# A second pair of token tiles by seven products, five tiles beside the attention, and PSUM dealt out anew

## The chip, the cores and the metric

One Trainium2 chip, one of its cores. The time is device microseconds of that core for one execution; lower is better. In this text and in the profile, PE is TensorE (PEld its weight loads), DVE is VectorE, ACT is ScalarE, POOL is GpSimd and SP is SyncE, which issues the DMAs.

## What is computed

A random-feature attention over 8 batches of 8 heads, 576 positions of 64, and then a gated MLP on its output, 4608 tokens of 512 with a hidden width of 1536. Cut to what matters:

```python
def phi(x):
    proj = einsum('bhsd,md->bhsm', x, omega)       # 128 features
    h = proj - sum(x * x, -1, keepdims=True) / 2
    h = h - max(h, -1, keepdims=True)
    return exp(h) / sqrt(m)
q_p, k_p = phi(q * scale), phi(k * scale)
kv = einsum('bhsm,bhsd->bhmd', k_p, v); z = sum(k_p, axis=2)
x = einsum('bhsm,bhmd->bhsd', q_p, kv) / (einsum('bhsm,bhm->bhs', q_p, z)[..., None] + 1e-6)
x = x.transpose(0, 2, 1, 3).reshape(4608, 512)
g = x @ w_gate
out = (g * sigmoid(g) * (x @ w_val)) @ w_out       # the weights come as float64
```

## The kernel before

**Precision.** Each MLP operand is split into a high half (a cast, on ACT) and a low half (a subtraction, on POOL or DVE), and each product is three matmuls: high by high, high by low, low by high. The weights arrive as float64 words; `convert_all` turns 36 pieces into float32 with one ACT, five DVE and one POOL operation each and keeps them in DRAM (`wscr`).

**The attention** runs in 72 steps of two groups of 256 rows: six steps of two k groups, sixty of one q and one k group, six of two q groups. A step projects its rows with omega (`st_project`, tile `pp`, L399), takes maxima on DVE (`st_max`), exponentials on ACT (`st_exp`, L431), and adds k's features to `kvacc` (`k_accumulate`, L534). Features of q are transposed (`q_transpose`, tile `ptq`, L558) and multiplied with kv (`q_out`, tile `xt`, L600 to L635; for the first four batches by way of `q_mult`, L575). Rows for the next step are transposed in `st_transpose` (tile `pt`, L376). `q_out` writes x, column by column, as high and low halves straight into the MLP's tiles (L632, L633).

**The MLP** takes tokens in nine tiles of 512 and the hidden width in four sets of three pieces. A visit is one tile by one set (`stream`, L689): three gate products (`g`, 12 matmuls each, 512 wide), Silu of the three on ACT (L714), the four down products of the visit before (`o`, 9 matmuls each, added up in SBUF by DVE, L680), three value products (`v`, 12 each, L647). That makes 108 wide matmuls. Three rounds of tiles, 0 to 2, 3 and 4, 5 and 6, are visited this way, 28 visits, beside the attention. Tiles 7 and 8 come after it as a pair (`last_round`): for each two pieces, a 2x2 block scheme with seven products in place of eight, whose weight factors come from `load_seven` and whose x factors `t1` to `t4` from `make_t`. A pair costs six times 14 products of 6 matmuls (`a`, `c`, `d`, L832) and 8 down products of 6.

**Order.** The program is emitted in a hand-made order. In each step the list `GROUPED` (L957) runs the attention's functions, with places named SHARE at which `give` lets the MLP's generator run on; how far is set by `course`, a curve of MLP microseconds over the steps, between an upper bound (what x is whole) and a lower one (what buffers of x must be free). `MARGIN` is what is left of the MLP's visits when the attention ends. `want` sets the conversions in the same way; `need` forces them where they are late. The engines' queues are in order, so a PE instruction that waits holds up all behind it.

**PSUM** has eight banks: four for the MLP (`ps_m`), two for `pp` and, from step 26 on, `pt` and `xt` (`ps_p`), one for `ptq`, `po` and `zp` (`ps_a`), one for `kvacc`. After the attention its four go to the pair's accumulators (`ps_w`). x has four buffers for each half (`NXB`).

Of the kernel before, what the change touches and what calls it, by code (L numbers as in the profile page):

```python
# [23 lines left out]
def kernel(  # L24
# [11 lines left out]
    nc = tc.nc  # L36
# [49 lines left out]
    ps_m = ctx.enter_context(tc.tile_pool(name="ps_m", bufs=4, space=PSUM))  # L86
# [3 lines left out]
    ps_a = late.enter_context(tc.tile_pool(name="ps_a", bufs=1, space=PSUM))  # L90
    ps_k = late.enter_context(tc.tile_pool(name="ps_k", bufs=1, space=PSUM))
# [4 lines left out]
    def ps_att(name, shape):  # L96
        return ps_a.tile(shape, F32, name=name, tag="b")

# [96 lines left out]
    lower = np.minimum(lower, upper)  # L195
# [44 lines left out]
    def new_weights(f, i, pool=None):  # L240
        hi, lo = (
            (pool or wpool).tile([P, DM], F32R, name=f"w{e}{f}_{i}", tag=f"w{e}{i}") for e in ("hi", "lo")
        )
        weights[f, i] = hi, lo
# [51 lines left out]
    def load_weights(f, i, pool=None):  # L296
        need(f, i)
        new_weights(f, i, pool)
        raw = moe.tile([P, DM], F32, name=f"wraw{f}_{i}", tag="wraw", bufs=3)
        nc.sync.dma_start(raw, wscr[f, i])  # L300
        split_piece(f, i, raw)
# [67 lines left out]
    def st_transpose(n):  # L369
# [3 lines left out]
        pt = (ps_moe if n <= EARLY else ps_proj)(f"pt_{n}", [P, 2, G])  # L373
# [89 lines left out]
    def load_z(n):  # L463

        for _, b, g, gr in slots(n, "q"):
            if g == 0 and b >= BPOOL:
                assert len(converted) == 3 * NF, "the raw weights' buffers are still needed"
                zt = att.tile([P, 2, 4, M], F32, name=f"zt{b}", tag="stw")
# [80 lines left out]
    def q_transpose(n):  # L549
# [3 lines left out]
        for b, g in todo:  # L553
            ph = box.pop(("q", b, g))
            pt = (ps_moe if m < EARLY else ps_att)(f"ptq{b}_{g}", [P, 2, G])
# [3 lines left out]
            qts[b, g] = att.tile([P, 2, G], F32, name=f"qt{b}_{g}", tag="qt")  # L559
# [34 lines left out]

    xt = {}
    cols_done = [0]

    def q_out(n):
        n -= OLAG
        for _, b, g, gr in slots(n, "q"):  # L600
            po = (ps_att if n + OLAG < EARLY else ps_proj)(f"xt{b}_{g}", [P, G])
# [56 lines left out]
    at_visit = [0]  # L658

    def finished(j):  # L660

        return at_visit[0] > last_visit[j]

# [3 lines left out]
    acc = {}  # L667

    def down(j, k_, ht, wts, next_set, tt):
# [11 lines left out]
        if k_ == (NPF if j >= LASTA else NSET) - 1:  # L681
# [7 lines left out]
    def stream():  # L689

        todo = []
        for vi, (j, s_, k_) in enumerate(visits):
# [4 lines left out]
            while not avail(j):  # L697
# [3 lines left out]
                else:  # L701
                    yield None
            xs = [t[:, :, 0:w] for t in xt[j]]
# [15 lines left out]
            if final:  # L719
                load_seven(0, 0)  # L720
            while todo:
                down(*todo.pop(0))
                yield MM2
            for f in fs:
# [13 lines left out]
            if final:  # L738
                load_seven(0, 1)
            at_visit[0] = vi + 1  # L740
            wts = {f: weights[f, 2] for f in fs} if vi else None
            then = range(nxt[1] * FA, nxt[1] * FA + FA) if new_set else (0, 1) if final else None
            todo = [(j, k_, ht, wts, then, tt) for tt in range(w // P)]
        yield from last_round(todo)
# [10 lines left out]

    late_pools = {}
    sevens = {}
    ts = {}

    def load_seven(pf, i):  # L760

        win = late_pools["win"]
        raws_ = []
        for f in (2 * pf, 2 * pf + 1):
            raw = moe.tile([P, DM], F32, name=f"wraw{f}_{i}s", tag="wraw", bufs=3)
            nc.sync.dma_start(raw, wscr[f, i])
            raws_.append(raw)
# [275 lines left out]
```

## Time and profile before

| | us |
|---|---|
| median of three runs (1230.67 to 1234.53) | 1233.17 |
| the profiled execution | 1232.11 |
| its span, first to last instruction | 1229.9 |
| PE busy | 1193.3 |
| ACT, DVE, POOL busy | 624.6, 607.8, 549.3 |
| mean granted clock of PE | 0.989 |

A row of a group gives line, engine, operation, the tile written, the tiles read, shape and count, then busy time, the mean of one in ns and the idle time before, with what ended it. A row of the timeline gives start and length in microseconds, and in brackets how long the engine was idle before and what released it. Matmuls overlap in the pipeline, so a PE row's length (0.39 for a wide one) is longer than the distance between two starts. A wait is put down to whatever came last.

### The profile page before, as it was taken

The page shows a single profiled execution, that of the slowest core. Times are in us where ns is not written, and L with a number is a line of the kernel's source. Part 1 is how long each engine was busy: PE and PEld are TensorE (multiplying, and loading weights), DVE is VectorE, ACT ScalarE, POOL GpSimd, SP SyncE. Part 2 cuts the span into 40 slices and gives each one's busy share as a digit, 9 for nine tenths or more (in the row PEclk, how much of TensorE's full clock was granted, in tenths as well). Part 3 has the DMA queues.
Part 4 walks back from the last instruction along what each step waited for, and adds up shares of the span by engine and source line. Part 5 has one row for each costly group of instructions (what it writes and reads, how often), then busy time and mean ns, then how long its engine had stood idle before and what let it go on. Part 6 is the DMA issues. An engine that isn't in the chain of part 4 may idle for free. (4 is left out here: it accounts for less than half of the span.)

```text
span 1229.9 us, 18546 instructions
## 1 busy us (share of the span) xinstructions
PE 1193.3 (97%) x6777; PEld 978.9 (80%) x6777; DVE 607.8 (49%) x1192; ACT 624.6 (51%) x1387; POOL 549.3 (45%) x469
## 2 busy tenths in 40 slices
PE   6999999899999999999999999989999999999998
PEld 5888788688888888878888877877777787788886
DVE  4688767436556523433344434432334276545544
ACT  3778766543544425455754556434654423654431
POOL 3424333353444521335544654335556334656541
PEclk7899999999999999999999999999999999999999
DMA  6545644424326312232222221222111113321102
GB/s 148 138 121 141 177 137 142 117 78 142 90 68 181 90 35 73 61 78 61 72 62 61 78 56 44 61 51 60 46 42 43 43 43 77 96 52 52 52 18 69
DMA packets 158986, 100.13 MB, mean 81 GB/s; under 512 B 119824, under 2 KB 132144, under 8 KB 158896
## 3 DMA queue, kind: packets, MB, share of 16 engines
q1 hardware_dynamic: 158896, 98.95, 30.1%
q8 instruction: 54, 0.88, 0.3%
q14 instruction: 36, 0.29, 0.1%
HBM read 80.02 MB, written 18.89 MB: 80 GB/s over the span
## 5 line engine op out<-in xcount | busy, mean ns | idle before, releaser
L431 ACT ACTIVATE ph<-pp,st 128x128 f32<-128x128 f32 x576 | 158.6, 382 | 31.8 <-DVE st L420 30.9
L249 POOL TENSOR_TENSOR wlo<-wraw,whi 128x512 fp32r<-128x512 f32 x93 | 121.8, 1319 | 107.5 <-ACT whi L248 107.1
L383 POOL TENSOR_TENSOR sq<-nat 128x512 f32<-128x512 f32 x72 | 76.7, 1066 | 191.9 <-DMA nat<-in_k_dram 143.2
L680 DVE TENSOR_TENSOR acc<-o,acc 128x512 f32<-128x512 f32 x124 | 84.6, 687 | 116.5 <-PE o L656 116.2
L656 PE MATMUL o<-whi,hh 128*128 128x512 f32 x336 | 135.5, 403 | 3.8 <-ACT hh L733 2.0
L647 PE MATMUL v<-xh,whi 128*128 128x512 f32 x336 | 134.5, 400 | 0.7 <-DVE acc L680 0.7
L647 PE MATMUL g<-xh,whi 128*128 128x512 f32 x336 | 134.6, 401 | 0.0
L656 PE MATMUL o<-whi,hl 128*128 128x512 f32 x336 | 132.3, 394 | 2.3 <-POOL hl L734 2.3
L647 PE MATMUL g<-xl,whi 128*128 128x512 f32 x336 | 131.7, 393 | 0.5 <-DVE xl L633 0.5
L656 PE MATMUL o<-wlo,hh 128*128 128x512 f32 x336 | 131.6, 392 | 0.0
L647 PE MATMUL v<-xh,wlo 128*128 128x512 f32 x336 | 131.4, 391 | 0.0
L647 PE MATMUL g<-xh,wlo 128*128 128x512 f32 x336 | 131.3, 392 | 0.0
L647 PE MATMUL v<-xl,whi 128*128 128x512 f32 x336 | 131.2, 391 | 0.0
L734 POOL TENSOR_TENSOR hl<-sl,hh 128x512 fp32r<-128x512 f32 x84 | 110.5, 1319 | 41.8 <-ACT hh L733 41.3
L417 DVE TENSOR_REDUCE st<-pp 128x4 f32<-128x512 f32 x144 | 93.5, 684 | 54.2 <-PE pp L399 54.2
L733 ACT CAST hh<-sl 128x512 fp32r<-128x512 f32 x84 | 52.1, 626 | 108.7 <-DVE sl L730 108.5
L248 ACT CAST whi<-wraw 128x512 fp32r<-128x512 f32 x93 | 57.4, 625 | 92.2 <-PE v L647 54.1
L410 DVE TENSOR_REDUCE st<-sq 128x8 f32<-128x512 f32 x72 | 49.1, 682 | 105.0 <-POOL sq L383 105.0
L399 PE MATMUL pp<-omT,x 64*128 64x128 f32 x1152 | 98.3, 296 | 2.4 <-ACT x L384 1.2
L399 PEld LDWEIGHTS pp<-omT,x 64*128 64x128 f32 x1152 | 81.2, 196 | 22.8 <-issue 13.9
L730 DVE TENSOR_TENSOR sl<-v,sl 128x512 f32<-128x512 f32 x84 | 57.3, 686 | 72.3 <-PE v L647 70.0
L494 POOL TENSOR_TENSOR jk<-ph,zt 128x512 f32<-128x512 f32 x32 | 41.1, 1290 | 103.6 <-ACT ph L431 86.8
(200 smaller groups left out, 2448.3 us busy)
## 6 DMA issues: line engine op xcount, KB each, us to landing
wraw<-wscr SPq DMA_DIRECT2D x93, 256.0 KB, 2.7
wscr<-wc SPq DMA_DIRECT2D x36, 256.0 KB, 2.2
out_dram<-acc SPq DMA_DIRECT2D x72, 128.0 KB, 2.4
nat<-in_k_dram SPq DMA_DIRECT2D x64, 128.0 KB, 3.3
v<-in_v_dram SPq DMA_DIRECT2D x64, 128.0 KB, 3.4
nat<-in_q_dram SPq DMA_DIRECT2D x64, 128.0 KB, 2.7
st<-in_moe_w_gate_dram SPq DMA_DIRECT2D x12, 512.0 KB, 5.1
st<-in_moe_w_val_dram SPq DMA_DIRECT2D x12, 512.0 KB, 4.4
```

The lines of the kernel that those rows point to most:

```text
L248: nc.scalar.copy(hi, raw)
L249: nc.gpsimd.tensor_tensor(lo, raw, hi.bitcast(F32), op=ALU.subtract)
L383: nc.gpsimd.tensor_tensor(sq, nat, nat, op=ALU.mult)
L399: nc.tensor.matmul(pp[hh][:, i, c, :], x[r, i, c * P : (c + 1) * P], omT[r], start=True, stop=True)
L417: nc.vector.tensor_reduce(st[:, 1, :, :, hh], pp[hh], axis=AX.X, op=ALU.max, negate=True)
L431: nc.scalar.activation(ph[:, c, hh * M : (hh + 1) * M], pp[hh][:, i, c, :], AF.Exp, bias=st[:, 3, i, c, hh : hh + 1], scale=1.0,)
L647: nc.tensor.matmul(ps, a_[:, ws], b_[:, c, :], start=n == 0, stop=n == 3 * NC - 1)
L656: nc.tensor.matmul(ps, a_[:, ts_], b_, start=first and n == 0, stop=last and n == 2)
L680: nc.vector.tensor_tensor(a_, po, a_, op=ALU.add)
L730: nc.vector.tensor_tensor(h, pv, h, op=ALU.mult)
L733: nc.scalar.copy(hh, h)
L734: nc.gpsimd.tensor_tensor(hl, h, hh.bitcast(F32), op=ALU.subtract)
```

## The change

Tiles 0 to 4 are visited beside the attention, in two rounds, 20 visits. Tiles 5 and 6 and then 7 and 8 are pairs by seven products, twelve pair visits; the second pair runs over the pieces backwards, so that the last weights serve twice. The x of tiles 3 to 8 goes to DRAM as plain float32 (`x_dram`); tiles 3 and 4 are fetched again before their round (`fetch_x`), the first pair's factors are made from DRAM as the attention ends (`first_x`), the second pair's raw factors are prepared ahead (`next_x`) and split during the last half visit of the first pair (`split_x`). With that x needs three buffers, the lower bound on the course and the forced `give` in `q_out` go, and the margin is 45.

PSUM: three banks for the MLP; one bank (`ps_b`) for `pt`, for the first `xt` of a step, and for the second `ptq` where a step has two; `pp` has its two banks to itself. Afterwards the pair has five banks and its down products three. `q_out` moves up between the halves of `k_accumulate`. Weights of the pair are fetched some products ahead (`weights_work`).

```diff
-    ROUNDS = [range(0, 3), range(3, 5), range(5, 7)]
-    LASTA, LASTB = 7, 8
-    MARGIN = 25.0
-    NXB = 4
+    ROUNDS = [range(0, 3), range(3, 5)]
+    PAIRS = [(5, 6), (7, 8)]
+    MARGIN = 45.0
+    NXB = 3
...
-    ps_m = ctx.enter_context(tc.tile_pool(name="ps_m", bufs=4, space=PSUM))
+    ps_m = ctx.enter_context(tc.tile_pool(name="ps_m", bufs=3, space=PSUM))
+    ps_b = late.enter_context(tc.tile_pool(name="ps_b", bufs=1, space=PSUM))
+    def ps_tr(name, shape):
+        return ps_b.tile(shape, F32, name=name, tag="t")
...
-        lower[n] = max([0.0] + [cum[last_visit[j - NXB] + 1] for j in begun if j >= NXB and begun[j] <= n])
...
-        pt = (ps_moe if n <= EARLY else ps_proj)(f"pt_{n}", [P, 2, G])
+        pt = ps_tr(f"pt_{n}", [P, 2, G])
...
-            pt = (ps_moe if m < EARLY else ps_att)(f"ptq{b}_{g}", [P, 2, G])
+            pt = (ps_moe if m < EARLY else ps_tr if i else ps_att)(f"ptq{b}_{g}", [P, 2, G])
...
-            po = (ps_att if n + OLAG < EARLY else ps_proj)(f"xt{b}_{g}", [P, G])
+            po = (ps_att if n + OLAG < EARLY or i else ps_tr)(f"xt{b}_{g}", [P, G])
...
+                if j in x_dram:
+                    xo = att.tile(list(src.shape), F32, name=f"xo{b}_{g}_{j}", tag="xo", bufs=3)
+                    nc.scalar.copy(xo, src)
+                    nc.sync.dma_start(x_dram[j][:, pr, o : o + w], xo)
+                    continue
                 if j not in xt:
-                    while j - NXB >= 0 and not finished(j - NXB):
-                        assert give(1), "the MLP waits for x, and x for the MLP"
...
+    def fetch_x(j):
+        xt[j] = [xres.tile([P, NPAIR, T], F32R, name=f"x{e}{j}", tag=f"x{e}") for e in "hl"]
+        for c in range(NC):
+            raw = moe.tile([P, T], F32, name=f"xraw{j}_{c}", tag="wraw", bufs=3)
+            nc.sync.dma_start(raw, x_dram[j][:, c, :])
+            hi, lo = (t[:, c] for t in xt[j])
+            nc.scalar.copy(hi, raw)
+            nc.gpsimd.tensor_tensor(lo, raw, hi.bitcast(F32), op=ALU.subtract)
...
+            if nxt and nxt[0] not in xt and avail(nxt[0]) and last_visit[nxt[0] - NXB] < vi:
+                fetch_x(nxt[0])
...
+    def split_x(name):
+        hi, lo = factors[name]
+        nc.scalar.copy(hi, ahead[name])
+        nc.vector.tensor_tensor(lo, ahead[name], hi.bitcast(F32), op=ALU.subtract)
...
+                    if new_x and i == 1:
+                        split_x(PROD[n][1])
...
         lambda n: k_accumulate(n, 0),
+        q_out,
         lambda n: k_accumulate(n, 1),
...
         lambda n: st_transpose(n + 1),
-        q_out,
         q_mult,
...
-        ("ps_w", tc.tile_pool(name="ps_w", bufs=4, space=PSUM)),
+        ("ps_w", tc.tile_pool(name="ps_w", bufs=5, space=PSUM)),
...
-    late_pools["mt"] = make_t()
-    for _ in late_pools["mt"]:
-        give(1.0)
+    new_factors()
+    for _ in first_x():
+        give(1.5)
```

What this makes of the order is shown at three places. First PE before, in step 65, at the end of the first visit of tile 5 (`v` and `o` are the value and down products of that same visit, `hh` and `hl` the split halves):

```order
L647 MATMUL v_2_8238<-xh_6028,whi_1_7332 128x512
L647 MATMUL v_2_8238<-xl_6029,whi_1_7332 128x512
L647 MATMUL v_2_8238<-xh_6028,wlo_1_7333 128x512
L656 MATMUL o_0_0_8256<-whi_2_7490,hh_0_8171 128x512
L656 MATMUL o_0_0_8256<-wlo_2_7491,hh_0_8171 128x512
L656 MATMUL o_0_0_8256<-whi_2_7490,hl_0_8172 128x512
L656 MATMUL o_0_0_8256<-whi_2_7496,hh_1_8234 128x512
```

And PE now, in step 59, where the second round begins with tile 3 (`xh_6292` and `xl_6293` are that tile's fetched halves, `ptq`, `kvacc` and `xt` the attention's):

```order
L566 MATMUL ptq_6_6384<-ident,ph_57_6131 128x128 x4
L542 MATMUL kvacc_0_6391<-v_97,ph_57_6136 128x65 x2
L623 MATMUL xt_5_6394<-qt_5_6238,kvr_0_4492 64x256 x2
L542 MATMUL kvacc_0_6391<-v_97,ph_57_6136 128x65 x2
L659 MATMUL g_9_6428<-xh_6292,whi_0_5136 128x512
L659 MATMUL g_9_6428<-xl_6293,whi_0_5136 128x512
L659 MATMUL g_9_6428<-xh_6292,wlo_0_5137 128x512
```

Before, the down products stand right behind the last value product of their own visit; now a gate product of the next tile follows, and `xt` stands between the halves of `kvacc`.

The second place is PE before where `pt` and `xt` of a step stood together between MLP units, in step 58:

```order
L647 MATMUL v_5_7298<-xh_4864,wlo_1_6705 128x512
L376 MATMUL pt_7312<-ident,nat_6932 128x128 x4
L613 MATMUL xt_4_7322<-qt_4_7080,kvr_0_5421 64x256 x2
L647 MATMUL g_0_7338<-xh_2566,whi_0_7113 128x512
L647 MATMUL g_0_7338<-xl_2567,whi_0_7113 128x512
```

The same place now, in step 59, between the second and the third gate product:

```order
L659 MATMUL g_10_6441<-xh_6292,whi_0_5142 128x512
L659 MATMUL g_10_6441<-xl_6293,whi_0_5142 128x512
L659 MATMUL g_10_6441<-xh_6292,wlo_0_5143 128x512
L385 MATMUL pt_6455<-ident,nat_6092 128x128 x4
L659 MATMUL g_11_6465<-xh_6292,whi_0_5148 128x512
```

`pt` stands there alone, in a bank of its own.

The third place is new: DVE in the last half visit of the first pair, where the second pair's factors are split (`b11lo`, `t1lo` and so on), between additions into the seven products' sums (`late_8880`), gating products (`sl1k`) and the down products' additions (`acc`):

```order
L841 TENSOR_TENSOR b11lo<-late_8876,b11hi 128x1024
L697 TENSOR_TENSOR acc_0_9285<-o_4_0_10241,acc_0_9285 128x512
L841 TENSOR_TENSOR t1lo<-late_8876,t1hi 128x1024
L971 TENSOR_TENSOR late_8880<-c_1_10221,late_8880 128x512
L841 TENSOR_TENSOR t2lo<-late_8877,t2hi 128x1024
L953 TENSOR_TENSOR sl1k<-late_8880,sl1k 128x512
L841 TENSOR_TENSOR b22lo<-late_8877,b22hi 128x1024
L697 TENSOR_TENSOR acc_1_9312<-o_4_1_10270,acc_1_9312 128x512
L971 TENSOR_TENSOR late_8880<-a_1_10220,late_8880 128x512
L841 TENSOR_TENSOR t3lo<-late_8878,t3hi 128x1024
```

The additions that empty `c` and `a` stand behind three and four of the wide subtractions.

More of the change, by code (lines that the diff above doesn't have):

```diff
@@ L294, in need, with load_weights, fetch @@
             tick()
-    def load_weights(f, i, pool=None):
+    def load_weights(f, i):
         need(f, i)
[L298 to L301, printed above, removed]
+        fetched = fetch((f,), i)
+        new_weights(f, i)
+        split_piece(f, i, fetched[0])
+    def fetch(fs, i):
+        raws_ = []
+        for f in fs:
+            raw = moe.tile([P, DM], F32, name=f"wraw{f}_{i}", tag="wraw", bufs=3)
+            nc.sync.dma_start(raw, wscr[f, i])
+            raws_.append(raw)
+        return raws_
     omT = const.tile([P, M], F32, name="omT")
@@ L466, in load_z @@
             if g == 0 and b >= BPOOL:
-                assert len(converted) == 3 * NF, "the raw weights' buffers are still needed"
-                zt = att.tile([P, 2, 4, M], F32, name=f"zt{b}", tag="stw")
+                zt = att.tile([P, 2, 4, M], F32, name=f"zt{b}", tag="zt")
                 for a2 in range(2):
@@ L595 @@
     xt = {}
+    x_dram = {j: dram.tile([P, NPAIR, T], F32, name=f"xs{j}") for j in range(NXB, len(TILES))}
     cols_done = [0]
@@ L875, in plus @@
                 def plus(n, ps, name):
[L876 removed]
+                    o = sl[n] if i == 0 else kp[:, 3]
                     nc.vector.tensor_tensor(o, ps, keep[name], op=ALU.add)
                     use(n, o)
[L880 to L883 removed]
```

272 lines of the change are left out of this document (156 added, 116 removed).

## The prediction

> **What bounds the kernel now.** I read the page's first part, then the busy time by stage, then what TensorE waits for, then the chain that ended last.
>
> ```profile
> span 1229.9 us, 18546 instructions
> PE 1193.3 (97%) x6777; PEld 978.9 (80%) x6777; DVE 607.8 (49%) x1192; ACT 624.6 (51%) x1387; POOL 549.3 (45%) x469
> ```
>
> TensorE is busy 97% of the span, no other engine, its own overlapping weight loads aside, over 51%. That is a mean over stages, so the stages follow: columns are length, then busy time of PE, weight loads, DVE, ACT and POOL, the granted clock, DMA. The cuts are the attention alone (0 to 130), its steps with little MLP (to 240), the MLP's forced stretch (to 440), attention with MLP between (to 950), the end.
>
> ```profile
> 0.00:130.00 130.00, 113.62 (x990) 102.28 (x991) 91.21 (x222) 89.96 (x271) 48.86 (x61) 0.91 0.57 141
> 130.00:240.00 110.00, 102.95 (x685) 85.19 (x684) 77.78 (x176) 68.97 (x167) 39.70 (x32) 1.00 0.51 145
> 240.00:440.00 200.00, 199.56 (x996) 165.10 (x995) 99.28 (x167) 86.87 (x166) 87.28 (x67) 1.00 0.34 101
> 440.00:950.00 510.00, 505.71 (x2898) 405.72 (x2897) 200.02 (x423) 267.22 (x585) 237.13 (x207) 1.00 0.23 58
> 950.00:1230.00 280.00, 271.50 (x1216) 220.62 (x1214) 139.47 (x206) 111.58 (x201) 136.33 (x105) 1.00 0.21 57
> ```
>
> From 130 us on PE has work in every stage and the others are at 71% or less, so the time is TensorE's instruction stream plus its few waits. Those, longest first in total:
>
> ```profile
> PE pt_om L312 <- DMA om<-in_omega_dram: 4.9, 1, 4.9
> PE pt L376 <- ACT ph L431: 3.8, 4, 2.5
> ...
> PE o L656 <- POOL hl L734: 2.3, 2, 1.3
> PE o L656 <- ACT hh L733: 2.0, 1, 2.0
> PE o L656 <- ACT sl L714: 1.7, 1, 1.7
> ...
> PE o L656 <- POOL hl0s L862: 0.9, 1, 0.9
> PE v L647 <- DVE acc L680: 0.7, 1, 0.7
> PE a L832 <- DVE c L877: 0.3, 1, 0.3
> ```
>
> A matmul removed is therefore worth its pitch. Busy times are pipelined and overlap, so the pitch comes from starts, in the chain that ended last (start, length, what):
>
> ```profile
> 1068.68 1.38 PE a L832 x6
> ...
> 1140.79 1.36 PE c L832 x6
> ```
>
> Between these two lie 53 groups of six matmuls 512 wide: 72.11 us by 318 is 0.227 us each.
>
> **The change part by part.** The sum is made against the profiled execution, 1232.11 us, which is its span of 1229.9 and 2.2 around it; the median of the runs, 1233.17, is 1.1 above it.
>
> *Matmuls.* A pair of tiles costs 2 x 4 visits x 108 = 864 wide matmuls in the plain way, and 6 x (14 x 6 + 48) = 792 by seven products. A second pair saves 72, all on the bound engine: 72 x 0.227 = **-16.3**. The order counts 3816 before and 3744 now.
>
> *The MLP that caught up with the attention.* Before, tiles 5 and 6 run beside the attention, and the first visit of their round ends before x of tile 6 is whole (step 66). The loop then takes the down products straight after the value products, whose split halves are not ready:
>
> ```profile
> 825.24 0.39 PE L656 MATMUL o<-wlo,hh 128*128 128x512 f32 x1
> 827.65 0.50 PE L656 MATMUL o<-whi,hh 128*128 128x512 f32 x1 [2.02 <-ACT hh L733]
> ...
> 829.70 1.22 PE L656 MATMUL o<-whi,hl 128*128 128x512 f32 x2 [1.31 <-POOL hl L734]
> 830.72 0.63 PE L656 MATMUL o<-whi,hh 128*128 128x512 f32 x1
> 831.14 0.63 PE L656 MATMUL o<-wlo,hh 128*128 128x512 f32 x1
> ...
> 833.18 0.60 PE L376 MATMUL pt<-ident,nat 128*128 128x128 f32 x4
> ```
>
> From 825.24 to 833.18 eleven matmuls start in 7.94 us where 11 x 0.227 = 2.50 would do: 5.4 lost, part of it after the waits at a pitch of 0.42 us (830.72 to 831.14), a slowed clock. The new list of five tiles asks for tiles 3 and 4 only after twelve visits, in step 59, when they have been whole since steps 43 and 48; no down product follows a value product of its own visit there. **-5.4**, at least 0.
>
> *One bank for the transposes of q and k.* From step 26 on pt took a bank of the projections, which the exponentials must first empty:
>
> ```profile
> 219.60 0.66 PE L376 MATMUL pt<-ident,nat 128*128 128x128 f32 x4 [2.47 <-ACT ph L431]
> ```
>
> Now it has its own, shared with xt, which is read out half a step earlier. Of the 3.8 us in the list of waits I take **-3**, between 0 and -3.8: next late there is ACT itself. *In the last steps, with two q groups each*, the second ptq and the first xt share that bank, so xt waits for a copy like this one:
>
> ```profile
> 611.41 0.58 ACT L560 COPY qt<-ptq 128x512 f32<-128x512 f32 x1 [0.57 <-PE ptq L558]
> ```
>
> Six such steps, 0 to 0.6 us each with what the scheduler puts between: 0 to +4, taken **+1**.
>
> *Three banks for the MLP instead of four.* Nothing of before shows three, but it shows when each bank was emptied. I set the start of each of 325 accumulators (g, v, o) against the end of the read-out of the third one before it, instead of the fourth. In 314 the read-out had ended. In eleven it had not, by 13.2 us together; these are the two largest:
>
> ```profile
> 303.78 0.39 PE L647 MATMUL v<-xh,whi 128*128 128x512 f32 x1
> ...
> 305.87 1.28 DVE L680 TENSOR_TENSOR acc<-o,acc 128x512 f32<-128x512 f32 x2
> ```
> ```profile
> 1023.59 0.50 PE L656 MATMUL o<-whi,hh 128*128 128x512 f32 x1 [1.66 <-ACT sl L714]
> ...
> 1025.91 2.48 DVE L680 TENSOR_TENSOR acc<-o,acc 128x512 f32<-128x512 f32 x4
> ```
>
> The value product at 303.78 would need the second of two additions, ending at 306.5; the down product at 1023.59 the first of four, ending at 1026.5. Eight of the eleven lie between 291 and 412 us, where DVE converts weights in bursts and hardly any attention lies between the MLP's units, three at the entry to the pair stage, none between 440 and 950:
>
> ```profile
> 350.00:400.00 50.00, 50.00 (x246) 41.62 (x246) 32.48 (x56) 22.32 (x43) 21.40 (x17) 1.00 0.41 121
> ```
>
> The new order spreads those conversions over steps 34 to 46 with attention in every gap, which takes most of them away and adds a few. 0 to +13.2; nearer the lower half: **+5**.
>
> *Edits with one answer.* Before step 25 the projections and ptq share three banks where they and pt shared four, so the cover is the same; xt moved up between the halves of the kv products, a fourth qt buffer and zt's own buffer change no count; 0, and if the early steps lose their cover, some tenths of a us in each of 25.
>
> *x through DRAM.* For tiles 3 to 8 one ACT copy replaces cast and subtraction, and a DMA goes onto SP's queue behind it, ahead of loads issued three steps early: nothing on PE. Tiles 3 and 4 come back in four chunks each, 256 KB, one cast and one POOL subtraction a chunk:
>
> ```profile
> L249 POOL TENSOR_TENSOR wlo<-wraw,whi 128x512 fp32r<-128x512 f32 x93 | 121.8, 1319 | 107.5 <-ACT whi L248 107.1
> ...
> L248 ACT CAST whi<-wraw 128x512 fp32r<-128x512 f32 x93 | 57.4, 625 | 92.2 <-PE v L647 54.1
> ...
> wraw<-wscr SPq DMA_DIRECT2D x93, 256.0 KB, 2.7
> ```
>
> 2.7 + 0.6 + 4 x 1.3 = 8.5 us, under three value products (36 x 0.227 = 8.2) and an attention group: 0 to +3 a tile, **+1** for both.
>
> *Entering the first pair.* Before, four waits there sum to 3.6 (sl 1.7, hl0s 0.9, acc 0.7, c 0.3). DVE now does 22 operations instead of 24, beneath 45 us of MLP instead of 25: -3.6 to +3.6, **-1**.
>
> *Entering the second pair* is new: while the last half visit runs, seven factors of 128x1024 are split again, each a cast and a DVE subtraction. The nearest DVE rows are half as wide, alone and beside a POOL instruction:
>
> ```profile
> 998.41 0.69 DVE L822 TENSOR_TENSOR t0l<-t1f,t0h 128x512 fp32r<-128x512 f32 x1
> ...
> 1002.43 1.77 DVE L822 TENSOR_TENSOR t1l<-t2f,t1h 128x512 fp32r<-128x512 f32 x1
> ```
>
> So 1.4 to 2.5 each, 10 to 17 us, and eleven other operations of 0.69 make 17 to 25 in a half visit of 11 x 6 x 0.227 = 15.0. Each factor is used only a half visit later, but product 4 waits for an addition queued behind those splits: 0 to +5, **+2**. [...]
>
> Sum: -16.3 - 5.4 - 3 + 1 + 5 + 1 - 1 + 2 = -16.7. Span 1213.2, execution 1215.4, median **1216.5**.
>
> **The rivals.**
>
> *Nothing new waits.* No bank wait, all old waits gone: -16.3 - 5.4 - 3.8 - 3.6 = -29.1, **1204**. For it: DVE and ACT are half idle. Against: conversions still come in bursts of 15 operations. Chance 0.17.
>
> *The seams take it back.* Banks at their bound (+13.2), second pair +5, fetched tiles +6, two-q steps +4 against -16.3 and -5.4: +6.5; with half of the last two +1.5, so **1235**, no change that a measurement of this kernel can tell (0.3%, some 3.7 us). For it: each has its row. Against: all must come together. 0.11.
>
> *Three banks stop PE in every visit (slower).* With three gates in three banks, the first down product needs the first Silu finished, where before it had the fourth bank. ACT may have exponentials and a table load ahead:
>
> ```profile
> 600.12 0.39 PE L656 MATMUL o<-whi,hh 128*128 128x512 f32 x1
> ...
> 599.80 0.91 ACT L431 ACTIVATE ph<-pp,st 128x128 f32<-128x128 f32 x3
> 600.73 1.28 ACT L714 ACT_TABLE_LOAD   x1
> 602.02 0.60 ACT L714 ACTIVATE sl<-g 128x512 f32<-128x512 f32 x1
> ```
>
> Had that been the first Silu, the down product at 600.12 would start 2.5 us late. A bank fewer moves each need forward by one accumulator, so where four just sufficed a visit loses 9 x 0.227 = 2.04 us: 20 visits, +40.8 in place of +5, **1252**. It decides from (21.7 + 3.7)/20 = 1.3 us a visit. Against it: none of the eleven late read-outs lies in the mixed stage, which most resembles the new one. Two short waits close together also slowed the clock at 830 (a pitch of 0.42), which would raise the price. 0.10. [...]
>
> **How the numbers follow.** Forecast 0.62 (1209 to 1224), rivals 0.17, 0.11, 0.10. Range 1204 to 1231: from the first rival to within the second. Faster than 1229.5: 0.62 + 0.17 + 0.03 = 0.82; within 0.3%: 0.08; slower: 0.10.
>
> **What would show it.** Right: 3744 wide matmuls, no PE wait of 2 us and no clock dip where the second round ends, fewer than 10 us of PE waiting on acc, sl or v's read-out, a pair stage at 0.227 throughout save the second pair's entry. Wrong: o or v waiting on ACT sl or DVE acc visit after visit, or a PE share under 95% after 240 us.

## The result, and the profile after

| | before | after |
|---|---|---|
| median, us (lowest to highest) | 1231.92 (1228.93 to 1234.53), 4 runs | 1218.27 (1217.01 to 1221.51), 4 runs |
| ratio after to before | | 0.9892, 95% interval 0.9872 to 0.9912 |
| the profiled execution, us | 1232.11 | 1217.01 |
| its span, us | 1229.9 | 1214.9 |
| wide matmuls | 3816 | 3744 |

The kernel became 1.1% faster; 1216.5 had been forecast. The page after has the same shape as before: TensorE at 97%, and no other engine above 54%, its own overlapping weight loads (79%) aside:

```profile
span 1214.9 us, 18839 instructions
PE 1173.3 (97%) x6705; PEld 965.4 (79%) x6705; DVE 646.2 (53%) x1231; ACT 656.6 (54%) x1461; POOL 584.9 (48%) x500
```

The last three of the same stages in the trace of after (length, busy time of PE, weight loads, DVE, ACT and POOL, the granted clock, DMA):

```profile
...
240.00:440.00 200.00, 189.11 (x1138) 154.90 (x1137) 124.89 (x228) 107.48 (x238) 94.40 (x75) 0.98 0.44 124
440.00:950.00 510.00, 503.24 (x2717) 404.70 (x2716) 216.88 (x402) 271.75 (x575) 270.57 (x231) 1.00 0.30 79
950.00:1215.00 265.00, 260.14 (x1147) 214.75 (x1145) 136.93 (x209) 113.77 (x198) 130.14 (x102) 1.00 0.20 53
```

One row has changed its nature. Before, PE was busy for 199.56 of the 200 us from 240 to 440; now it is for 189.11, and DVE has 124.89 us to do there where it had 99.28. The list of what PE waits for, in the trace of after, says on whom:

```profile
PE pp L408 <- ACT x L393: 5.6, 7, 2.1
...
PE pt L385 <- ACT xo L638: 4.4, 3, 2.7
...
PE ptq L566 <- DVE xn L593: 3.2, 2, 1.8
PE a L874 <- DVE sl2k L971: 3.2, 1, 3.2
PE pt L385 <- DVE xl L645: 2.5, 3, 1.9
...
PE a L874 <- ACT late L967: 1.5, 2, 1.2
PE o L668 <- ACT sl L733: 1.4, 1, 1.4
PE v L659 <- DVE acc L697: 1.3, 2, 1.1
PE o L668 <- DVE acc L697: 1.2, 1, 1.2
```

`pt` no longer waits for the exponentials `ph`; it waits for `xo` and `xl`, the two read-outs of `xt`, which now shares its bank. The waits on hh and hl of the visit's own, where the second round ended, are gone. The three banks show as sl and acc: 1.4 + 1.3 + 1.2 = 3.9 us.

To compare kernels I cut their traces at the same steps of the attention, not at the same times; the start of a step is taken from its copy of x out of `pt` (L393). The idle time of PE that ends on another engine or a DMA is added up for each part:

| steps | before | after |
|---|---|---|
| 0 to 24 | 16.1 | 13.8 |
| 24 to 35 | 7.4 | 4.8 |
| 35 to 50 | 0.2 (242 to 589 us) | 11.1 (237 to 456 us) |
| 50 to 68 | 3.8 | 2.0 |
| 68 to the end | 3.6 | 4.9 |
| all | 31.1 | 36.6 |

Steps 35 to 50 are where the change gives something back. They lasted 347 us and last 219 now, because the MLP no longer has to run ahead there to free a buffer of x; the same attention and the same conversions of weights stand in a shorter stretch. A second sum, the start of the last wide matmul less 0.2268 us for each wide matmul, holds all that isn't wide matmuls on time: 359.3 us before, 360.9 after. So the 72 matmuls (16.3 us) are the whole gain, and everything else comes out at +1.6 us, of gains and losses that the experiments take apart in part.

### The profile page after: what moved, and what is told of

Same layout as the page of the kernel before. It is cut to its first block, busy times and chain, and to the rows that moved or that the text cites. A ratio compares the mean times of both kernels' runs of the same rounds, so it can differ in the third digit from the quotient of the medians.

```text
span 1214.9 us, 18839 instructions
## 1 busy us (share of the span) xinstructions
PE 1173.3 (97%) x6705; PEld 965.4 (79%) x6705; DVE 646.2 (53%) x1231; ACT 656.6 (54%) x1461; POOL 584.9 (48%) x500
## 4 chain that ended last, share of the span: by engine, by line
PE 59%; DVE 5%; DMA 3%; POOL 2%; issue 2%; ACT 1%; SPq 0%; POOLq 0%; DVEq 0%; ACTq 0%
PE o L668 19%; PE a L874 10%; PE v L659 7%; PE g L659 7%; PE c L874 5%; PE d L874 2%; PE pp L408 2%; PE kvacc L542 2%; PE xt L623 1%; PE ptq L566 1%; DMA nat<-in_k_dram 1%; PE pt L385 1%; DMA first_b<-xs 1%; POOL jk L502 0%; DVE wc L276 0%
## 5 line engine op out<-in xcount | busy, mean ns | idle before, releaser
L426 DVE TENSOR_REDUCE st<-pp 128x4 f32<-128x512 f32 x144 | 92.7, 682 | 24.2 <-PE pp L408 23.7
L668 PE MATMUL o<-whi,hh 128*128 128x512 f32 x240 | 97.1, 405 | 2.6 <-ACT sl L733 1.4
L408 PEld LDWEIGHTS pp<-omT,x 64*128 64x128 f32 x1152 | 77.8, 196 | 26.4 <-issue 13.8
L659 PE MATMUL v<-xh,whi 128*128 128x512 f32 x240 | 96.7, 403 | 1.3 <-DVE acc L697 1.3
L659 PE MATMUL g<-xh,wlo 128*128 128x512 f32 x240 | 95.1, 396 | 0.0
L668 PE MATMUL o<-wlo,hh 128*128 128x512 f32 x240 | 94.3, 393 | 0.0
L668 PE MATMUL o<-whi,hl 128*128 128x512 f32 x240 | 94.1, 392 | 0.2 <-POOL hl L756 0.2
L659 PE MATMUL v<-xh,wlo 128*128 128x512 f32 x240 | 94.0, 392 | 0.0
L659 PE MATMUL v<-xl,whi 128*128 128x512 f32 x240 | 93.7, 390 | 0.0
L280 POOL TENSOR_TENSOR wc<-st,wc 128x512 f32<-128x512 f32 x36 | 47.5, 1321 | 80.2 <-DVE wc L278 27.8
L865 POOL TENSOR_TENSOR wlo<-s,whi 128x512 fp32r<-128x512 f32 x44 | 64.8, 1489 | 34.6 <-DVE late L971 11.7
L865 POOL TENSOR_TENSOR wlo<-wraw,whi 128x256 fp32r<-128x256 f32 (+1 forms) x44 | 45.1, 1025 | 72.0 <-ACT whi L864 71.9
```

Of the source, the lines that this page charges most:

```text
L408: nc.tensor.matmul(pp[hh][:, i, c, :], x[r, i, c * P : (c + 1) * P], omT[r], start=True, stop=True)
L426: nc.vector.tensor_reduce(st[:, 1, :, :, hh], pp[hh], axis=AX.X, op=ALU.max, negate=True)
L659: nc.tensor.matmul(ps, a_[:, ws], b_[:, c, :], start=n == 0, stop=n == 3 * NC - 1)
L668: nc.tensor.matmul(ps, a_[:, ts_], b_, start=first and n == 0, stop=last and n == 2)
L865: nc.gpsimd.tensor_tensor(lo, src_, hi.bitcast(F32), op=ALU.subtract)
```

## The experiments

Each kernel is one edit away from before, from after, or from another experiment. Line numbers in their traces are shifted by a few lines. Waits are those of PE in the profiled execution, in us.

| kernel | median | ratio to before (95%) | all waits | steps 35 to 50 |
|---|---|---|---|---|
| after | 1218.27 | 0.9892 (0.9872 to 0.9912) | 36.6 | 11.1 |
| psum_only | 1229.56 | 0.9983 (0.9963 to 1.0003) | 33.2 | 8.1 |
| pair_only | 1235.02 | 1.0040 (1.0014 to 1.0066) | 44.0 | 14.0 |
| pair_three | 1238.28 | 1.0063 (1.0036 to 1.0089) | 45.2 | 13.8 |
| q_late | 1232.61 | 1.0007 (0.9986 to 1.0027) | 45.2 | 13.4 |
| pair_qup | 1243.24 | 1.0100 (1.0071 to 1.0130) | 55.2 | 19.7 |
| xt_att | 1244.60 | 1.0095 (1.0069 to 1.0121) | 47.7 | 18.3 |
| q_first | 1220.08 | 0.9915 (0.9889 to 0.9940) | 39.5 | 8.0 |
| conv_light | 1202.01 | 0.9765 (0.9733 to 0.9797) | 32.7 | 1.0 |
| no_catchup | 1226.48 | 0.9956 (0.9937 to 0.9975) | 27.2 | 0.2 |
| prep_late | 1221.79 | 0.9911 (0.9883 to 0.9938) | 38.0 | 9.1 |
| prep_pool | 1221.86 | 0.9910 (0.9877 to 0.9943) | 36.7 | 11.4 |
| combo1 | 1266.12 | 1.0267 (1.0229 to 1.0304) | 66.0 | 24.3 |

### The two halves of the change, apart

**psum_only** is before with the PSUM dealt out anew and `q_out` moved up, and with no second pair:

```diff
-    ps_m = ctx.enter_context(tc.tile_pool(name="ps_m", bufs=4, space=PSUM))
+    ps_m = ctx.enter_context(tc.tile_pool(name="ps_m", bufs=3, space=PSUM))
+    ps_b = late.enter_context(tc.tile_pool(name="ps_b", bufs=1, space=PSUM))
...
-        pt = (ps_moe if n <= EARLY else ps_proj)(f"pt_{n}", [P, 2, G])
+        pt = ps_tr(f"pt_{n}", [P, 2, G])
...
-            po = (ps_att if n + OLAG < EARLY else ps_proj)(f"xt{b}_{g}", [P, G])
+            po = (ps_att if n + OLAG < EARLY else ps_tr)(f"xt{b}_{g}", [P, G])
```

> The kernel before with PSUM dealt out as now, and nothing else but q_out moved up: three banks for the MLP, one for pt and xt, five and three banks in the pair stage. Theory A (the new deal costs: late read-outs with three banks up to 13.2 us, most in the MLP's forced stretch, and pt now waits for the read-out of xt, against 3.8 us of waits on the exponentials that go): slower than before by 3 to 10 us, 1235 to 1242, with PE waits on acc, sl and v's read-out of 4 us or more between 240 and 440 us. Rival B (the deal is the gain: with pp's banks to itself the early steps run ahead, as the changed kernel reached step 24 6 us earlier): faster by 3 to 8 us, 1224 to 1229, with step 24 reached near 124 us.

**pair_only** is the opposite: after with the three lines above, the pair's banks and the place of `q_out` as they were before.

> The changed kernel with PSUM as before (four banks for the MLP, pt and xt in the projections' banks, four banks for the pair) and q_out in its old place: the second pair alone. Theory A: 72 matmuls and the stall at the second round's end go (-21.7), the new PSUM deal isn't paid: 1208 to 1214, and the PE waits on acc and sl between 250 and 440 us (3.7 us in the changed kernel) are gone, with those on xo and xl. Rival B: without the deal's gain 1221 to 1226.

Theory A was right about the waits in both, and about the time in neither. In psum_only PE waits for the third bank where the late read-outs had been found. The longest of these waits, at 302.63 us, is this row; 1.9 and 1.3 us follow at 381.31 and 389.04, 7.8 in all:

```profile
PE v L651 <- DVE acc L684: 4.6, 1, 4.6
```

Rival B fell as well: step 24 starts at 128.5 us, where it starts at 125.5 in before and at 124.1 in after. In pair_only the waits on acc and sl are gone, with those of `pt` on xo and xl. Still the deal by itself is worth nothing that can be told (0.9983, interval up to 1.0003), and the second pair by itself is slower than before (1.0040), although it has its 72 matmuls fewer. Only together do they give 1.1%. In the list of waits of pair_only one row stands out:

```profile
PE pt L381 <- ACT ph L436: 18.5, 11, 4.8
```

Before, the same transposes in the same banks waited 3.8 us for the same exponentials. What changed is what lies over them: 13.1 of the 18.5 us fall in steps 35 to 50, where before had no such wait, and these steps are shorter by a third. Their granted clock is 0.96, where it was 1.00.

**no_catchup** prices the stall at 825 us in before: the MLP hands out no early down products while x of tile 6 is not whole.

```diff
-                if todo:
+                if todo and j != 6:
```

> The kernel before with one edit: while x of tile 6 isn't whole, the MLP hands out nothing, where it handed out the down products of the visit just done. Theory A (the stall at 825 us costs 5.4): no wait on hh and hl and no clock dip there, 4 to 6 us faster than before. Rival B (the attention step left without MLP work costs as much, since PE then waits for the step's own chain): within 2 us of before.

The stall and the dip of the clock behind it (granted 0.50 from 831 to 833 us in the trace of before) are gone; 0.9956 of 1230.83 is 5.4 us less (3.1 to 7.8).

**pair_three** takes the fourth MLP bank from pair_only and leaves it unused.

```diff
-    ps_m = ctx.enter_context(tc.tile_pool(name="ps_m", bufs=4, space=PSUM))
+    ps_m = ctx.enter_context(tc.tile_pool(name="ps_m", bufs=3, space=PSUM))
```

> The second pair with PSUM as before, but three banks for the MLP during the attention and the pair stage, one bank left unused: it prices the fourth bank alone. Theory A (three banks cost little once attention lies between the MLP's units; what made the old deal slow here are the 18.5 us for which pt waits for exponentials): within 4 us of the old deal's 1235, that is 1233 to 1240, and pt still waits 12 us or more. Rival B (the MLP's banks matter as much as my bound of 13.2): 1243 to 1250, with over 8 us of PE waits on acc, sl and v's read-out.

1238.28 against 1235.02: the fourth bank is worth some 3 us; the intervals, 1.0036 to 1.0089 and 1.0014 to 1.0066, overlap, so it may be less. No visit after visit of waiting came with it.

### Who makes PE wait in steps 35 to 50

**conv_light** is after with one DVE operation for each converted piece of weights instead of five. It leaves out the clamp and the bit operations, so that the weights are other numbers; the MLP's work is otherwise the same.

```diff
-            nc.vector.tensor_scalar(u, u, E_LO, E_HI, op0=ALU.max, op1=ALU.min)
...
-            nc.vector.tensor_scalar(ui, ui, 3, 0x3FFFFFFF, op0=ALU.logical_shift_left, op1=ALU.bitwise_and)
...
-            nc.vector.scalar_tensor_tensor(ri, ri, -0x40000000, ui, op0=ALU.bitwise_and, op1=ALU.bitwise_or)
...
-            nc.vector.tensor_single_scalar(ui, ri, -0x800000, op=ALU.bitwise_and)
```

> The changed kernel with one DVE operation in place of five for each converted weight piece (the conversion's range and bit operations are left out, so the weights are other numbers). Theory A (the 10.9 us of PE waits between 255 and 431 us come from conversions queued on DVE and ACT in steps 34 to 46): those waits fall under 4 us and the time by 7 to 12, to 1206 to 1211. Rival B (they come from three banks and the shared bank of pt and xt, whatever DVE does): the waits stay over 7 us and the time falls by under 4.

The waits of these steps go from 11.1 to 1.0 us and the time to 1202.01. So it is DVE's part of the conversions that makes PE wait there; DVE is busy for 93.36 us of these steps, in after for 133.42. The time falls by 16 us, more than these 10. The start is not where it comes from: the first wide matmul starts at 125.1 us, that of after at 130.8, but at step 35 conv_light is only 0.6 us ahead (236.2 and 236.8), since `pt` waits 6.8 us for xl before it. Steps 35 to 50 then take 204.6 us in place of 218.9. Of these 14.3 us 10.1 are waits, and the rest goes with a granted clock of 1.00 where after has 0.98.

**combo1** tries to make use of that in a kernel that still computes everything: the clamp goes to POOL (and the subtractions of prep_pool, below, too).

```diff
-            nc.vector.tensor_scalar(u, u, E_LO, E_HI, op0=ALU.max, op1=ALU.min)
+            nc.gpsimd.tensor_scalar(u, u, E_LO, E_HI, op0=ALU.max, op1=ALU.min)
```

> The changed kernel with the preparing subtractions on POOL and, of the five DVE operations of a weight's conversion, the first one (the clamp) on POOL as well. Theory A (the waits in steps 35 to 50, 11.1 us, come from DVE's queue): DVE has some 36 operations less, those waits fall to 5 to 9 and the time by 4 to 8 with the second pair's wait, to 1210 to 1214. Rival B (the conversion's chain or POOL takes its place): those waits stay at 10 or more, the time at 1214 to 1220.

It is the slowest of all, 1266.12. The groups of POOL and of DVE in its trace show why (busy time, mean ns; idle time before them and on what):

```profile
L270 POOL TENSOR_SCALAR wc<-wc 128x512 f32<-128x512 f32 x36 | 70.6, 1961 | 43.9 <-ACT wc L268 43.8
```
```profile
L272 DVE TENSOR_SCALAR wc<-wc 128x512 int32<-128x512 int32 x36 | 33.3, 924 | 75.9 <-POOL wc L270 73.4 <-DMA xs<-xo 2.5
```

On DVE, in the trace of after, the clamp is this group:

```profile
L270 DVE TENSOR_SCALAR wc<-wc 128x512 f32<-128x512 f32 x36 | 22.2, 617 | 20.9 <-ACT wc L268 20.7
```

An operation of 617 ns became one of 1961, and the next one on DVE waits 73.4 us in total for it, with the attention's maxima behind. DVE's own work fell, from 646.2 to 629.4 us; its queue got later, and not in steps 35 to 50 alone: of the 54.6 us between the two profiled executions 33.3 are lost by step 35. (The other edit in this kernel is harmless by itself, as prep_pool shows below.)

### The bank and the place of q_out

In after, `pt` waits for `xt`'s read-out, 6.9 us. **xt_att** gives `xt` another bank, that of `ptq` and `po`:

```diff
-            po = (ps_att if n + OLAG < EARLY or i else ps_tr)(f"xt{b}_{g}", [P, G])
+            po = ps_att(f"xt{b}_{g}", [P, G])
```

> The kernel after, with one edit: every xt goes to the bank of ptq, po and zp, so that pt shares its bank with nothing but the second ptq of the last steps. In the kernel after pt waits 4.4 us for the copy of xt to xo and 2.5 us for the subtraction to xl. Theory A: these 6.9 us are the price of the shared bank; they go, and PE gains 3 to 6 us with the slowed clock behind them: 1212 to 1215. Theory B: the price is the lateness of ACT and DVE among the conversions, whichever bank xt has; the waits move to ptq and po (ptq or po on xo or xl, 5 us or more together), and the time stays within 1216 to 1222. Between the two the sum of all PE waits decides: 36.6 in the kernel after, under 32 by A, over 34 by B.

**q_late** puts `q_out` back behind the next step's transposes:

```diff
         lambda n: k_accumulate(n, 0),
-        q_out,
         lambda n: k_accumulate(n, 1),
...
         lambda n: st_transpose(n + 1),
+        q_out,
         q_mult,
```

> The kernel after, with one edit undone: q_out stands behind the next step's transposes again, as before the change, instead of between the halves of the kv products. The prediction put this move at nothing. Theory A: the move is what makes one bank for pt and xt possible; with xt right behind pt in the same bank, xt must wait for the copy of pt (some 0.6 us on ACT behind what is queued there) in up to 48 steps, where MLP products in between do not hide it: xt shows waits on x of 4 us or more in total, and the time is 1222 to 1232. Theory B: the MLP's products lie between in nearly all steps, pt no longer waits for xo and xl, and the two balance: 1214 to 1221.

In xt_att both theories fell: the waits did move, but to `xt` itself, which stands right behind `ptq` in the bank and waits for the copy qt, 19.9 us in total, and the time is 1244.60. In q_late A was right: 19.3 us of waits on x, and 1232.61, just past its range. The lists of waits, first of xt_att, then of q_late:

```profile
PE xt L616 <- ACT qt L568: 12.7, 7, 3.6
PE xt L623 <- ACT qt L568: 7.2, 2, 4.1
```
```profile
PE xt L616 <- ACT x L393: 10.9, 7, 4.3
PE xt L623 <- ACT x L393: 8.4, 6, 5.3
```

One of these waits, followed back in the timeline of q_late. PE stops at 369.96 with 8 of 12 matmuls of `g` to go, because `xt` needs the bank of `pt`:

```profile
367.56 0.60 PE L385 MATMUL pt<-ident,nat 128*128 128x128 f32 x4
...
369.56 0.40 PE L659 MATMUL g<-xh,whi 128*128 128x512 f32 x1
374.28 0.44 PE L616 MATMUL xt<-ident,xn 128*128 128x128 f32 x2 [4.32 <-ACT x L393]
```

ACT empties `pt` only after the step's eight exponentials, and has itself been idle for 3.30 us, waiting for DVE:

```profile
371.58 2.17 ACT L440 ACTIVATE ph<-pp,st 128x128 f32<-128x128 f32 x8 [3.30 <-DVE st L429]
373.59 0.63 ACT L393 COPY x<-pt 128x512 f32<-128x512 f32 x1
```

And DVE comes to the maxima (L426) and to L429 among operations of the conversion (L270 to L278, two of them shown):

```profile
366.97 0.68 DVE L274 SCALAR_TENSOR_TENSOR st<-st,wc 128x512 int32<-128x512 int32 x1
...
368.02 1.28 DVE L426 TENSOR_REDUCE st<-pp 128x4 f32<-128x512 f32 x2
369.22 0.68 DVE L278 SCALAR_TENSOR_TENSOR wc<-st,wc 128x512 f32<-128x512 uint32 x1
...
370.23 1.25 DVE L429 SCALAR_TENSOR_TENSOR st<-st 128x8 f32<-128x8 f32 x1
```

So the rule of these three kernels: a bank that PE needs again, and that is given back behind the step's exponentials, is waited for by 18 to 31 us in total, 13.1 to 19.7 of it in steps 35 to 50. In pair_only it is `pp`'s bank, which the exponentials read; in q_late it is `pt`'s, whose copy stands behind them on ACT. In after neither `pt` nor `xt` stands behind them: `xt` follows a copy of x that was made half a step earlier, and the copy of x that does stand behind them is wanted only by the next step's `pp`, which waits 1.3 us for it in steps 35 to 50.

**pair_qup** closes the square: pair_only with `q_out` moved up.

```diff
         lambda n: k_accumulate(n, 0),
+        q_out,
         lambda n: k_accumulate(n, 1),
...
-        q_out,
         q_mult,
```

> pair_only (the second pair with the PSUM of before: four MLP banks, pt and xt in pp's two banks) plus the move of q_out between the halves of the kv products, as the kernel after has it. pair_only took 1235.0 and had PE waiting 18.5 us in pt for the exponentials; the kernel after with q_out in its old place took 1232.6. Theory A: the move alone is what was worth 14 us, in either deal, since it puts work between the transposes and the next step: pt's 18.5 us fall under 8 and the time comes to 1217 to 1224, so that the new deal of PSUM would be worth little. Theory B: the move pays only with the bank of pt's own; here pt still needs a bank of pp, which the exponentials empty, wherever xt stands: 14 us or more of waits for ph remain and the time is 1229 to 1238, so that deal and move are one edit worth some 14 us together and nothing apart.

B was right, and too mild: 1243.24. With a bank of `pp`, `xt` itself now waits for the exponentials, earlier in the step than `pt` did:

```profile
PE xt L619 <- ACT ph L436: 16.6, 10, 5.5
PE xt L612 <- ACT ph L436: 14.1, 8, 3.6
```

| second pair, with | q_out in its old place | q_out moved up |
|---|---|---|
| the PSUM of before | 1235.0 (pair_only) | 1243.2 (pair_qup) |
| the PSUM of after | 1232.6 (q_late) | 1218.3 (after) |

By itself the new PSUM gives 2.4 us, which can't be told from nothing (the intervals of pair_only and q_late overlap), and the move loses 8.2; together they give 16.7. **q_first** goes one place further in the same direction, ahead of `q_transpose`:

```diff
+        q_out,
         q_transpose,
         lambda n: k_accumulate(n, 0),
-        q_out,
         lambda n: k_accumulate(n, 1),
```

> The kernel after with q_out moved up once more, ahead of q_transpose instead of between the halves of the kv products, so that xt is read out earlier still before the next pt needs its bank. Theory A: pt's waits for xo and xl (4.4 and 2.5 us in the kernel after) come from the shortness of that gap; they fall under 2 us and the time is 1212 to 1217. Theory B: the gap was taken from the other side: xt now comes sooner after x is read out of the bank and after xn is made, so xt waits on x or xn by 4 us or more, as xt waited 19.3 us on x with q_out in its old place, and the time is 1218 to 1226.

The waits of `pt` on xo and xl fall from 6.9 to 0.7 + 1.2 = 1.9 us, as A had it, but the time doesn't: 1220.08, and the interval overlaps that of after. The list of its waits shows what came in their place:

```profile
PE pp L408 <- ACT x L393: 8.3, 8, 2.1
...
PE ptq L566 <- POOL hl L756: 2.8, 1, 2.8
PE o L668 <- DVE acc L697: 2.7, 1, 2.7
PE o L668 <- ACT sl L733: 2.6, 2, 2.2
```

Neither theory's row: xt on x does not appear, xt on xn is 2.5. In steps 35 to 50 all waits fall from 11.1 to 8.0 us, and elsewhere they rise from 25.5 to 31.5. It looks as if the lateness is DVE's and ACT's and shows at the next places once the shared bank is relieved; no run shows that by itself.

### The entry to the second pair

In after PE waits 3.19 us at 881.77 for an addition on DVE. This is in the first pair, 138 us before the second pair's first product (1019.28). DVE's timeline there:

```profile
873.29 1.28 DVE L850 TENSOR_TENSOR s<-wraw 128x256 f32<-128x256 f32 x1 [5.25 <-DMA wraw<-wscr]
...
875.62 1.28 DVE L829 TENSOR_TENSOR late<-late,late 128x512 f32<-128x512 f32 x2
876.83 1.28 DVE L829 TENSOR_TENSOR late<-late 128x512 f32<-128x512 f32 x2
878.03 0.68 DVE L971 TENSOR_TENSOR sl0k<-c,late 128x512 f32<-128x512 f32 x1
878.63 2.48 DVE L829 TENSOR_TENSOR late<-late,late 128x512 f32<-128x512 f32 x4
881.04 0.68 DVE L971 TENSOR_TENSOR sl2k<-a,late 128x512 f32<-128x512 f32 x1
```

These are the eight subtractions of `next_x` (L829), which prepare the second pair's raw factors. They come in one block, and the last of their loads was issued late: it stood on SP's queue behind three fetches of weights, which took 8.92 us to issue while SP waited for their buffers:

```profile
861.97 8.92 SPq L308 DMA_DIRECT2D wraw<-wscr  x3
870.94 0.43 SPq L825 DMA_DIRECT2D late<-xs  x1
```

**prep_late** lets nine more units pass before the subtractions and one between each two.

```diff
-        yield
+        for _ in range(9):
+            yield
...
                 nc.vector.tensor_tensor(ahead[o][:, c], ahead[a][:, c], ahead[b][:, c], op=ALU.subtract)
                 yield
+                yield
```

> The changed kernel with the eight DVE subtractions that prepare the second pair's factors begun a pair visit later and one to every second down product, their DMAs where they were. Theory A (the 3.2 us wait of product 4 at 881 us is due to the eight subtractions in one block ahead of its addition): that wait goes, the time falls by 2.5 to 4, to 1214 to 1216. Rival B (it is due to the weights' DMA, late behind the 2 MB for those factors, on which DVE stood for 5.25 us just before): the wait stays over 2 us, the time within 1.5 of the changed kernel's.

Inconclusive: the wait on sl2k is 3.2 us as before. The block on DVE stayed whole; the emission was spread, the instructions weren't. That fits the late load as the reason for the block; no run moves the load alone.

**prep_pool** puts the eight on POOL.

```diff
-                nc.vector.tensor_tensor(ahead[o][:, c], ahead[a][:, c], ahead[b][:, c], op=ALU.subtract)
+                nc.gpsimd.tensor_tensor(ahead[o][:, c], ahead[a][:, c], ahead[b][:, c], op=ALU.subtract)
```

> The changed kernel with the eight subtractions that prepare the second pair's factors on POOL instead of DVE. Theory A (product 4 waits 3.2 us because four of them stand ahead of its addition on DVE): the wait on sl2k goes, the time falls by 2 to 4, to 1214 to 1217. Rival B (DVE is late because it stood 5.3 us for the next weights' DMA): the wait stays over 2 us and the time with it.

The wait on sl2k is gone, although DVE stood 5.25 us for a load just before, as in after; so the block on DVE was its cause. But another wait comes half a visit later. POOL has the eight subtractions until 888.3 us and frees the weights' buffers later, DVE then stands 12.35 us for a fetch of weights, and PE waits for DVE's next addition:

```profile
892.41 0.63 DVE L850 TENSOR_TENSOR s<-wraw 128x256 f32<-128x256 f32 x1 [12.35 <-DMA wraw<-wscr]
```
```profile
897.45 0.50 PE L874 MATMUL a<-t4hi,whi 128*128 128x512 f32 x1 [1.79 <-DVE late L971]
```

From step 68 on the waits fall from 4.9 to 3.1 us, but the stretch takes 515.6 us in both kernels: seven of the matmuls behind the new wait start 0.43 us apart. The median can't tell the two apart: 1221.86, 0.9910 (0.9877 to 0.9943).

None of the kernels that compute the whole is faster than after.

## Why the prediction was right, and where its steps failed

- **Matmuls, -16.3: right.** 3744 wide ones, and in the pair stage six still take 1.36 us from start to start, 0.227 each:

```profile
911.98 1.36 PE a L874 x6
913.34 1.36 PE o L668 x6
```

- **The MLP that caught up, -5.4: right**, in cause and in size: no_catchup measured -5.4 (-3.1 to -7.8), and after has no such stall.
- **One bank for the transposes, -3: the step that failed.** Where it looked, in steps 24 to 35, the waits did fall by 2.6 us. But it priced the bank by the 3.8 us that the trace of before shows, a wait measured under the cover of before (the MLP's matmuls that keep PE busy meanwhile), and the same change takes that cover away: with the old banks `pt` waits 18.5 us in pair_only. The deal and the move of `q_out` together are worth 16.7 us, and in after `pt` still waits 6.9 us on xt's read-outs. "Next late there is ACT itself" was true, and had no price.
- **`q_out` moved up, 0: wrong.** It stood among the edits with one answer. It decides 14.3 us (q_late), as it sets what stands between one use of a bank and the next. The forecast came out only because it had assumed after to have no such waits, which is what the move does.
- **Three banks, +5: right in size, and the reason given holds for these waits.** psum_only, with three banks in the order of before, has 7.8 us of waits on acc and sl between 302 and 389 us, where eight of the eleven late read-outs had been found. In after, with the conversions spread, 3.9 are left, 3.7 of them between 386 and 431 us; pair_three prices the fourth bank at some 3 us. What the reason left out is the attention: with less MLP over the conversions its own waits grow, and steps 35 to 50 have 11.1 us in all where 0.2 had been.
- **Two-q steps, +1, and x through DRAM, +1: 0.** No wait in after at those six steps' shared bank, nor at the fetched tiles.
- **First pair, -1: some -2.** Of the four waits 0.24 us is left, on acc at 804.23, and a new one comes in the pair's first visit: 1.16 us at 861.65 for a read-out by ACT that stands behind two casts of weights.
- **Second pair, +2: 3.2 us, by another mechanism.** Splitting, which the term was about, runs from 1006.7 to 1022.5 us, and PE waits for nothing there; the seven subtractions took 1.21 to 1.23 us each, below the 1.4 to 2.5 allowed, with POOL idle until 1014.55. (Of the two rows behind that estimate the 0.69 was not quite alone either: a POOL instruction begins 0.18 us into it, at 998.59.) The 0.33 us at 1053.77 comes 31 us after the splitting. Preparing costs 3.19 us, at 881.77: `next_x` runs beside the first pair, and the sum had no term for it.
- **The rivals.** *Nothing new waits* fell with the 11.1 us. *The seams* had the right kind of loss in the wrong places. *Three banks stop PE in every visit* fell: from 240 us on PE is busy 189.11 + 503.24 + 260.14 of 975, 97.7%.

So the sum, -16.7 against -15.1 between the two profiled executions, is right with terms in it that failed, and that it came so close is in part luck. Beside the matmuls it had -0.4, and the second sum above gives +1.6. By stage that sum (the length less 0.2268 us for each wide matmul, up to the start of the last) changes so:

| steps | 0 to 24 | 24 to 35 | 35 to 50 | 50 to 68 | 68 to the end |
|---|---|---|---|---|---|
| change, us | -1.4 | -7.1 | +13.9 | -3.8 | 0.0 |

Steps 35 to 50 gave back nearly three times the 5 that were allowed: 10.9 of the 13.9 are waits, and the granted clock there is 0.98 where it was 1.00. In steps 50 to 68 the stall is gone, -5.4, of which 3.3 were waits (2.02 + 1.31) and 2.1 were lost behind them, where the granted clock fell to 0.50; a wait of 1.97 at 519.95 is new. Before step 35 after gains 8.5 us, of which 4.9 are waits of the lists, and no term had foreseen more than 3. That gain is not shown to be the change's: prep_late and prep_pool run the same instructions up to there, and by the same sum they take 188.3 and 186.0 us for them where after's profiled execution took 181.9 and that of before 190.2.

## What to carry to other kernels

A wait in the trace of before is a price under the cover of before: when a change takes work out of a stage, price every wait of that stage again, with what will then lie over it. For each PSUM bank ask behind what its release stands in the queue of the engine that empties it; two uses of a bank on either side of a late chain (here conversion, maxima, exponentials, copy) made PE wait 18 to 31 us in three kernels, by different tiles. With the new banks a line moved in the order is worth nearly as much as the matmuls saved (14.3 and 16.3 us); with the old ones the same move cost 8.2. In combo1 an operation of 617 ns on DVE, moved to POOL, where it took 1961, made DVE's queue later, not freer.

## What the runs showed of the hardware

**The clock slowed behind an idle of 2.67 us, and not behind one of 3.19.** In after PE idles for 2.67 us at 366.69, and then starts seven matmuls 0.43 us apart before it is back at 0.23, 1.4 us lost on top; the granted clock was 0.50 from 368 to 371 us:

```profile
366.69 0.66 PE L385 MATMUL pt<-ident,nat 128*128 128x128 f32 x4 [2.67 <-ACT xo L638]
...
368.54 0.63 PE L659 MATMUL g<-xl,whi 128*128 128x512 f32 x1
368.96 0.63 PE L659 MATMUL g<-xh,wlo 128*128 128x512 f32 x1
...
371.45 0.39 PE L659 MATMUL g<-xh,wlo 128*128 128x512 f32 x1
371.68 0.39 PE L659 MATMUL g<-xh,whi 128*128 128x512 f32 x1
```

After the 3.19 us at 881.77, in the same trace, the pitch is 0.23 from the second matmul on, and the granted clock was 1.00 from 881 to 885 us:

```profile
881.77 0.50 PE L874 MATMUL a<-t4hi,whi 128*128 128x512 f32 x1 [3.19 <-DVE sl2k L971]
882.10 0.39 PE L874 MATMUL a<-t4lo,whi 128*128 128x512 f32 x1
882.33 0.40 PE L874 MATMUL a<-t4hi,wlo 128*128 128x512 f32 x1
```

So the first wait cost half as much again, and the second 0.1 us more than itself. The length alone does not decide it: behind the wait of 3.2 us at the same product seven wide matmuls start some 0.43 us apart in conv_light and eight in q_first, and in after none. What does decide it, no run shows. Counted over the traces, 13 wide matmuls of after and 38 of q_late start in such stretches (three or more in a row, 0.38 to 0.48 us apart). At 0.2 us each that is some 5 us, part of why q_late takes 14.3 us longer with only 8.6 us more of waits.

**The granted clock of the first 80 us differs from one execution to another.** In stretches of 20 us it was 0.85, 0.73, 0.87 and 0.96 in before and 1.00, 1.00, 0.91 and 1.00 in after. In prep_late, which runs the same instructions as after up to there, it was 1.00, 1.00, 0.57 and 1.00, and step 24 starts at 131.4 us, in after at 124.1. Stages are therefore better compared by their own starts than by the time on the clock.
